# Reordering the products of a fast-matrix-multiply expert loop: y4 placed behind the next pair's two opening products

## The chip, the cores and the metric

The kernel runs on one core of one Trainium2 chip. The time is the device time of one execution in microseconds; shown is the median of several runs. The profile is one further execution, taken by the hardware profiler. TensorE is called PE, VectorE DVE, ScalarE ACT, GpSimd POOL and SyncE SP.

## The reference

A linear attention makes x, and a mixture of eight experts, all of them applied to every token, makes the output:

```python
def _attn_ref(q, k, v):                     # 8 batches, 8 heads, 576 tokens, 64 wide
    q_p, k_p = phi(q), phi(k)               # phi(x) = elu(x) + 1
    kv = np.einsum('bhsd,bhse->bhde', k_p, v)
    num = np.einsum('bhsd,bhde->bhse', q_p, kv)
    den = np.einsum('bhsd,bhd->bhs', q_p, np.sum(k_p, axis=2))[..., None] + 1e-06
    return num / den

def _moe_ref(x, w_gate, w1, w2):            # x 4608 x 512, w1 8 x 512 x 1024, w2 8 x 1024 x 512
    P = np.exp(x @ w_gate - max)            # then 8 rounds of normalising rows and columns
    out = 0
    for e in range(8):
        h = np.maximum(x @ w1[e], 0.0)
        out += P[:, e:e + 1] * (h @ w2[e])
    return out
```

## The kernel before, in words

**Stages.** The attention part, the routing weights P and expert 0 fill the first 206 us. Expert 0 uses plain products of 512 columns (`layer1`, line 546, and `unit_plain`, line 736). Experts 1 to 7 follow. The 4608 tokens are cut into nine groups of 512; one expert on one group is a **unit**, numbered u = 9 e + g, so units 9 to 71 are those of experts 1 to 7. Both layers of a unit are written as a fast matrix multiply in which seven block products take the place of eight. The last unit (71) has the fast form in its first layer only.

**First layer, `block7` (line 603).** It makes h (128 x 8 x 512, f16) in two halves, `pair(0)` and `pair(1)`, called a and b here. Each half has seven products a1 to a7 (b1 to b7). A product is four matmuls of 256 columns, all issued on line 640. Three PSUM banks take the sums:

- X (shown as `hq`, two buffers): product 1, then 6, 7 and 4 on top of it
- R (shown as `att`, two buffers): product 5, then 3
- Z (shown as `Zye`, one bank): product 2 on top of a copy of product 1

Between them ACT copies X after product 1 into Z (the seed, line 652), R after 5 into s5 (line 660) and X after 6 into s2 (line 656), and it makes h11 from Z after 2 (line 663) and h21 from X after 4 (line 666). DVE makes h12 from R and s2 after 3, and h22 from X and s5 after 7 (line 669, issued from lines 672 and 675; the task of h22 is `d22`). Product 4 overwrites what h22 reads, so it waits for h22. DVE also makes the sums W and T of the next expert's weights (lines 783 and 795), one in most units, directly behind h22 of pair b.

**Second layer, `unit` (line 800).** DVE forms four sums S0 to S3 of h (line 816), S0 once all of h is there. Then come seven products y1 to y7 of eight matmuls of 256 columns each (line 843). The bank X of this layer (`ye0`) takes y1, y6, y7 and y4 in that order, R (`ye1`) takes y5 and y3, and Z takes y2 on a copy of y1 (line 878). After y5, y6, y3, y7 and y4 the sum is read out by two DVE instructions each, which add P times it to the output accumulator `acc` (line 857); y2 is read out by ACT into `st` (line 864) and added by POOL (line 867). The next product into the same bank waits for these. y5 needs S0, y6 S1, y7 S2 and y3 S3.

**What sets the order.** Every piece of work is a task of the planner `_Plan` with an estimated time, dependencies, buffers to take and a rank (`prio`, the lowest first). `run()` is a greedy simulation: the engine that can start earliest takes, among the tasks that can start then, the one with the lowest rank, and emits it. So the queue of each engine is fixed when the program is built. On the chip each engine works through its queue and waits on semaphores. Rank for a unit ui: evictions and h11, h12, h21 ui - 400, h22 ui - 402, S ui - 399. On PE the planner has no choice from unit 9 on: `order` (line 919) is a list by hand, and each product is made dependent on the one before it in the list (line 927). A name with y in it means unit u - 1, a and b mean unit u, and a capital A means pair a of unit u + 1. So three units are woven into each other. `final` is the list of the last unit.

**Buffers.** There are two buffers of h. A planner task `tha` (line 612) takes one for a unit. It can be taken when the unit two before has been used for the last time, that is after its last y product. In the kernel before, the first product (`m1`, line 676) waits for `tha` in the plan, although it doesn't touch h. x comes from DRAM in blocks of 896 KB, two buffers, loaded by SP (line 598). The weights are loaded by POOL.

Of the kernel before, what the change touches and what calls it, by code (L numbers as in the profile page):

```python
# [17 lines left out]
class _Plan:  # L18
# [14 lines left out]
    def add(self, eng, fn, deps=(), prio=0.0, acq=(), use=(), lat=0.0, after=0.0):  # L33

        if isinstance(eng, tuple):
            eng = {eng[0]: eng[1]}
        k = len(self.t)
        t = {"eng": eng, "fn": fn, "prio": prio, "acq": tuple(acq), "lat": lat, "kids": [], "nd": 0,
             "ready": after, "done": None, "id": k}
        self.t.append(t)  # L40
        for d in set(x for x in deps if x is not None):
            self.t[d]["kids"].append(k)
            t["nd"] += 1
        for g in list(acq) + list(use):
            g["users"].append(k)
        return k
# [76 lines left out]
def kernel(  # L123
# [28 lines left out]
    add = S_.add  # L152
# [367 lines left out]
    prev_hq = [None]  # L520
# [72 lines left out]
    def x_load(e, g):  # L593
        gr = S_.grp(p_xs)

        def fn(_):
            gr["tile"] = accp[1].tile([P, NXB], FP16, tag="xs", name="xs")
            nc.sync.dma_start(out=gr["tile"], in_=xd[g])
        ti = add(("sp", 0.1), fn, acq=[gr], deps=xd_done[g] + [t_close, xs_prev[0]], prio=e * NG + g)
        xs_prev[0] = ti  # L600
        return gr, add(("dma", 3.0), lambda _: None, deps=[ti], use=[gr], prio=e * NG + g, lat=2.6)

    def block7(e, g, gW, tW):
        gw1, tw1, gw2, tw2 = w_t[e]
        ui = e * NG + g
        gxs, txs = x_load(e, g)
        gh = S_.grp(p_h)
        th = [[], []]

        def f_ha(_):  # L610
            gh["tile"] = hpool.tile([P, NFT, 512], FP16, tag="h", name="h")
        tha = add(("none", 0.0), f_ha, deps=[prev_hq[0]], acq=[gh], prio=ui - 400.0)

        def A(i, j, gi):
            return lambda p, c: gw1["tile"][:, 2 * (j - 1) + c, ts(4 * (i - 1) + 2 * gi + p, P)]

        def W(i, gi):
            return lambda p, c: gW["tile"][:, i - 1, c, ts(2 * gi + p, P)]

        def Bx(o, w):  # L620
            return lambda c: gxs["tile"][:, o + w * c:o + w * c + 256]

        def T(i):
            return Bx(1536 + 512 * (i - 1), 256)
        B11, B21, B22 = Bx(0, 256), Bx(512, 512), Bx(768, 512)

        def pair(gi):
            gX, gR, gZ, gs2, gs5 = (S_.grp(p) for p in (p_hq, p_att, p_ye[3], p_s2, p_s5))
            kx = {id(gX): (hqp, "hq"), id(gR): (aps, "att")}
            f0 = 2 * gi  # L630

            def pm(lhs, rhs, g_, first, deps, pr):
                def f_m(_):
                    if first:
                        pl, tag = kx[id(g_)]
                        g_["tile"] = pl.tile([P, 2, 256], FP32, tag=tag, name=tag)
                    dst = Zt[1] if g_ is gZ else g_["tile"]
                    for p in range(2):
                        for c in range(2):
                            nc.tensor.matmul(dst[:, p, :], lhsT=lhs(p, c), rhs=rhs(c),  # L640
                                             start=(first and p == 0 and c == 0), stop=(c == 1), skip_group_check=True)
                return add(("pe", 0.436), f_m, deps=deps, acq=[g_] if first else [], use=[g_, gw1, gW, gxs],
                           prio=ui + (0.35 if ui > NG else -2.0) + 0.35 * gi + pr)

            def hd(fh, t):
                return gh["tile"][:, 4 * fh + f0:4 * fh + f0 + 2, 256 * t:256 * t + 256]

            def acts(fn, deps, use, acq=()):
                return add(("act", 0.6), fn, deps=deps, use=use, acq=acq, prio=ui - 400.0 + 0.1 * gi)

            def f_seed(_):
                nc.scalar.copy(out=Zt[1], in_=gX["tile"])  # L652

            def f_s2(_):
                gs2["tile"] = accp[2].tile([P, 2, 256], FP32, tag="s2", name="s2")
                nc.scalar.copy(out=gs2["tile"], in_=gX["tile"])  # L656

            def f_s5(_):
                gs5["tile"] = accp[2].tile([P, 2, 256], FP32, tag="s5", name="s5")
                nc.scalar.copy(out=gs5["tile"], in_=gR["tile"])  # L660

            def f_h11(_):
                nc.scalar.activation(out=hd(0, 0), in_=Zt[1], func=AF.Relu)  # L663

            def f_h21(_):
                nc.scalar.activation(out=hd(1, 0), in_=gX["tile"], func=AF.Relu)  # L666

            def addrelu(dst, ps, sb):
                nc.vector._custom_dve(TENSOR_ADD_SAT, out=dst, in0=ps, in1=sb, s0=3.0e38, s1=0.0)  # L669

            def f_h12(_):
                addrelu(hd(0, 1), gR["tile"], gs2["tile"])

            def f_h22(_):
                addrelu(hd(1, 1), gX["tile"], gs5["tile"])
            m1 = pm(A(1, 1, gi), B11, gX, True, tw1 + [tha, txs, prev_hq[0]], 0.0)
            prev_hq[0] = m1
            a1 = acts(f_seed, [m1], [gX], [gZ])
            m5 = pm(W(1, gi), T(1), gR, True, [m1, tW], 0.05)
            a5 = acts(f_s5, [m5, x_closed[0]], [gR], [gs5])  # L680
            m2 = pm(A(1, 2, gi), B21, gZ, False, [a1], 0.15)
            th[0].append(acts(f_h11, [m2], [gZ, gh]))
            m6 = pm(W(2, gi), T(2), gX, False, [a1, tW], 0.08)
            a2 = acts(f_s2, [m6, x_closed[0]], [gX], [gs2])
            m3 = pm(W(4, gi), B22, gR, False, [a5], 0.12)
            th[1].append(add(("dve", 0.69), f_h12, deps=[m3, a2], use=[gR, gs2, gh], prio=ui - 400.0))
            m7 = pm(W(3, gi), T(3), gX, False, [a2], 0.14)
            d22 = add(("dve", 0.69), f_h22, deps=[m7, a5], use=[gX, gs5, gh], prio=ui - 402)
            th[1].append(d22)
            m4 = pm(A(2, 2, gi), T(4), gX, False, [d22], 0.16)  # L690
            for n, t in zip("1234567", (m1, m2, m3, m4, m5, m6, m7)):
                pe_id[(ui, f"{'ab'[gi]}{n}")] = t
            pe_id[(ui, f"{'ab'[gi]}22")] = d22
            th[0].append(acts(f_h21, [m4], [gX, gh]))
        pair(0)
        pair(1)
        return gh, th

# [211 lines left out]
    for e in range(1, E):  # L910
# [3 lines left out]
        for g in range(NG):  # L914
            if e == E - 1 and g == NG - 1:
                unit_plain(e, g, *co[0:2])
            else:
                unit(e, g, *co)
    order = "y1 y5 y2 y6 a7 y3 y7 a4 b1 b5 y4 b6 b3 b2 b7 A1 A5 b4 A6 A3 A2".split()
    final = "y1 y5 y2 y6 a7 y3 a4 b1 b5 y7 b6 b3 b2 b7 y4 b4".split()  # L920
    chain = []
    for u in range(NG - 1, E * NG):
# [83 lines left out]
```

## Time and profile before

| | us |
|---|---|
| median of 11 runs | 977.93 |
| lowest and highest | 976.04, 980.7 |
| profiled execution, its own time | 979.73 |
| profiled execution, span from first to last instruction | 977.9 |
| matmuls of the expert loop (line 843) from, to | 205.9, 966.2 |
| mean granted TensorE clock | 0.998 |

| engine | busy us | share |
|---|---|---|
| PE | 965.2 | 99% |
| PE's weight loads (PEld) | 794.5 | 81% |
| DVE | 768.2 | 79% |
| ACT | 569.3 | 58% |
| POOL | 111.7 | 11% |

The profile gives each instruction a start, a length, the line that issued it and the tiles that it writes and reads (`out<-in`). A matmul's record of 256 columns is 272 ns long, and the next one starts before it ends. Idle time of an engine is listed with what ended it. The chain of waits follows the program back from its last instruction, at each step to what released it.

### The profile page before, as it was taken

What the parts mean: (1) busy time and instruction counts of PE and PEld (TensorE: products, weight loads), DVE (VectorE), ACT (ScalarE), POOL (GpSimd) and SP (SyncE); (2) the same over time, 40 slices, a digit from 0 to 9 for tenths busy, and PEclk for the clock granted to TensorE, in tenths of its full rate; (3) what the DMA queues carried; (4) which work ended last, traced back from release to release, by engine and by line L of the source; (5) the groups of instructions that cost most, each with busy time, mean ns of one, the idle gap of its engine ahead of it and who ended that gap; (6) DMA issues with size and microseconds to landing.
All of it is one profiled execution on the core that took longest, in us unless ns stands there. A gap on an engine that the chain in (4) does not pass through costs nothing.

```text
span 977.9 us, 21442 instructions
## 1 busy us (share of the span) xinstructions
PE 965.2 (99%) x8737; PEld 794.5 (81%) x8737; DVE 768.2 (79%) x1563; ACT 569.3 (58%) x1049; POOL 111.7 (11%) x158
## 2 busy tenths in 40 slices
PE   8899999999999999999999999999999999999998
PEld 4556564588888888888888888888888888888886
DVE  6699868987777777777777777777777777777775
ACT  6699945565555555555555555555555555555553
POOL 3000000101111111111111111111111111111110
PEclk9999999999999999999999999999999999999999
DMA  9886926472226222272226322272225322236664
GB/s 316 231 291 220 252 58 229 157 149 73 73 78 139 93 74 76 73 160 77 76 76 141 95 76 76 77 162 76 77 76 132 107 77 76 76 97 165 161 162 109
DMA packets 47188, 121.99 MB, mean 125 GB/s; under 512 B 4208, under 2 KB 18288, under 8 KB 47088
## 3 DMA queue, kind: packets, MB, share of 16 engines
q1 hardware_dynamic: 32208, 99.76, 30.8%
q0 software_dynamic: 14480, 20.33, 11.7%
q8 instruction: 68, 1.11, 0.5%
q10 hardware_dynamic: 400, 0.52, 0.2%
q14 instruction: 32, 0.26, 0.1%
HBM read 119.69 MB, written 17.69 MB: 140 GB/s over the span
## 4 chain that ended last, share of the span: by engine, by line
PE 91%; DMA 4%; ACT 3%; DVE 1%; issue 1%; POOL 0%; SPq 0%; ACTq 0%; DVEq 0%; POOLq 0%
PE ye L843 33%; PE hq L640 23%; PE att L640 11%; PE ye L736 6%; PE Zye L640 6%; PE Zye L843 6%; PE hq L546 4%; DMA w<-in_moe_w_dram 2%; DMA kin<-in_k_dram 1%; ACT eq L266 1%; PE xt_ps L390 1%; DMA qin<-in_q_dram 1%; PE num_ps L374 1%; ACT h L550 1%; ACT ek L266 0%
## 5 line engine op out<-in xcount | busy, mean ns | idle before, releaser
L857 DVE SCALAR_TENSOR_TENSOR acc<-ye,P_sb,acc 128x256 f32<-128x256 f32 x620 | 264.9, 477 | 95.4 <-PE ye L843 78.7
L640 PEld LDWEIGHTS <-W 128*128 128x128 f16 x2016 | 197.0, 98 | 24.1 <-issue 0.2
L843 PEld LDWEIGHTS <-S 128*128 128x128 f16 x1984 | 194.1, 98 | 22.5
L843 PE MATMUL ye<-T,S 128*128 128x256 f16 x1488 | 192.8, 273 | 0.0
L666 ACT ACTIVATE h<-hq 128x512 f16<-128x512 f32 x126 | 76.4, 606 | 160.1 <-PE hq L640 160.1
L640 PEld LDWEIGHTS <-w 128*128 128x128 f16 x1512 | 147.6, 98 | 23.1 <-issue 0.8
L843 PEld LDWEIGHTS <-h 128*128 128x128 f16 x1488 | 145.6, 98 | 16.9
L867 POOL TENSOR_TENSOR acc<-acc,st 128x256 f32<-128x256 f32 x124 | 87.5, 725 | 625.6 <-ACT st L864 620.7
L640 PE MATMUL hq<-xs,W 128*128 128x256 f16 x1008 | 151.2, 273 | 0.1
L640 PE MATMUL att<-xs,W 128*128 128x256 f16 x1008 | 151.1, 272 | 0.0
L640 PE MATMUL hq<-xs,w 128*128 128x256 f16 x1008 | 140.7, 272 | 0.4 <-DVE h L669 0.3
L816 DVE TENSOR_TENSOR S<-h 128x1024 f16<-128x1024 f16 x124 | 85.3, 688 | 58.2 <-ACT h L666 58.2
L864 ACT ACTIVATE st<-Zye,P_sb 128x256 f32<-128x256 f32 x124 | 52.1, 471 | 78.3 <-PE Zye L843 78.3
L656 ACT COPY s<-hq 128x512 f32<-128x512 f32 x126 | 75.0, 595 | 36.7 <-PE hq L640 36.7
L669 DVE CUSTOM_DVE_ANT_0 h<-att,s 128x512 f16<-128x512 f32 x126 | 86.6, 687 | 11.5 <-ACT s L656 11.0
L663 ACT ACTIVATE h<-Zye 128x512 f16<-128x512 f32 x126 | 75.2, 597 | 34.8 <-PE Zye L640 34.8
L669 DVE CUSTOM_DVE_ANT_0 h<-hq,s 128x512 f16<-128x512 f32 x126 | 86.4, 686 | 0.1
L652 ACT COPY Zye<-hq 128x512 f32<-128x512 f32 x126 | 73.2, 581 | 17.5 <-PE hq L640 17.5
L736 PE MATMUL ye<-w,h 128*128 128x512 f16 x312 | 76.9, 383 | 3.4 <-DMA w<-in_moe_w_dram 2.8
L640 PE MATMUL Zye<-xs,w 128*128 128x256 f16 x504 | 75.6, 273 | 0.0
L660 ACT COPY s<-att 128x512 f32<-128x512 f32 x126 | 74.5, 591 | 0.0
L546 PE MATMUL hq<-xT,w 128*128 128x512 f16 x288 | 70.3, 379 | 1.0 <-ACT h L550 0.8
(95 smaller groups left out, 961.4 us busy)
## 6 DMA issues: line engine op xcount, KB each, us to landing
xs<-xd SPq DMA_DIRECT2D x63, 896.0 KB, 4.6
w<-in_moe_w_dram POOLq DMA_DIRECT2D x14, 1024.0 KB, 11.5
out_dram<-acc SPq DMA_DIRECT2D x67, 128.0 KB, 2.4
kin<-in_k_dram SPq DMA_DIRECT2D x14, 576.0 KB, 5.5
qin<-in_q_dram SPq DMA_DIRECT2D x14, 576.0 KB, 5.5
vin<-in_v_dram SPq DMA_DIRECT2D x14, 576.0 KB, 6.1
xd<-xst SPq DMA_DIRECT2D x9, 512.0 KB, 2.8
xd<-xT SPq DMA_DIRECT2D x9, 256.0 KB, 3.2
```

What stands on the lines that cost most here:

```text
L546: nc.tensor.matmul(ghq["tile"], lhsT=gw1["tile"][:, c, ts(f, P)], rhs=xT[:, c, ds(512 * g, 512)], start=(c == 0), stop=(c == NDT - 1))
L640: nc.tensor.matmul(dst[:, p, :], lhsT=lhs(p, c), rhs=rhs(c), start=(first and p == 0 and c == 0), stop=(c == 1), skip_group_check=True)
L656: nc.scalar.copy(out=gs2["tile"], in_=gX["tile"])
L660: nc.scalar.copy(out=gs5["tile"], in_=gR["tile"])
L663: nc.scalar.activation(out=hd(0, 0), in_=Zt[1], func=AF.Relu)
L666: nc.scalar.activation(out=hd(1, 0), in_=gX["tile"], func=AF.Relu)
L669: nc.vector._custom_dve(TENSOR_ADD_SAT, out=dst, in0=ps, in1=sb, s0=3.0e38, s1=0.0)
L736: nc.tensor.matmul(gy[tt]["tile"], lhsT=gh["tile"][:, f, ds(P * tt, P)], rhs=gw2["tile"][:, f, :], start=(f == 0), stop=(f == NFT - 1))
L816: nc.vector.tensor_tensor(out=Sx[:, i], in0=a0, in1=a1, op=op)
L843: nc.tensor.matmul(bank(g_)[:, s, :], lhsT=lhs(s, kk), rhs=rhs(kk), start=(new and s == 0 and kk == 0), stop=(kk == 3), skip_group_check=True)
L857: nc.vector.scalar_tensor_tensor(out=dst(), in0=bank(g_)[:, s, :], scalar=P_sb[:, gg, e:e + 1], in1=dst(), op0=ALU.mult, op1=ALU.add)
L867: nc.gpsimd.tensor_tensor(out=dst(), in0=dst(), in1=gst["tile"], op=ALU.add)
```

## The change

The list `order` is made anew. Three things move in it: y4 of the unit before goes from behind b5 to behind A5 (of the next unit); y7 goes from behind y3 to behind b5; a7 goes in front of y6. a4 follows y3 directly then. `final` stays as it is. With this list A1 of unit u + 1 comes ahead of y4 of unit u - 1, whose h buffer it would have to wait for in the plan. So `m1` no longer depends on `tha`; the four tasks that write h (`f_h11`, `f_h12`, `f_h22`, `f_h21`) do in its place.

```diff
-            m1 = pm(A(1, 1, gi), B11, gX, True, tw1 + [tha, txs, prev_hq[0]], 0.0)
+            m1 = pm(A(1, 1, gi), B11, gX, True, tw1 + [txs, prev_hq[0]], 0.0)
...
-            th[0].append(acts(f_h11, [m2], [gZ, gh]))
+            th[0].append(acts(f_h11, [m2, tha], [gZ, gh]))
...
-            th[1].append(add(("dve", 0.69), f_h12, deps=[m3, a2], use=[gR, gs2, gh], prio=ui - 400.0))
+            th[1].append(add(("dve", 0.69), f_h12, deps=[m3, a2, tha], use=[gR, gs2, gh], prio=ui - 400.0))
...
-            d22 = add(("dve", 0.69), f_h22, deps=[m7, a5], use=[gX, gs5, gh], prio=ui - 402)
+            d22 = add(("dve", 0.69), f_h22, deps=[m7, a5, tha], use=[gX, gs5, gh], prio=ui - 402)
...
-            th[0].append(acts(f_h21, [m4], [gX, gh]))
+            th[0].append(acts(f_h21, [m4, tha], [gX, gh]))
...
-    order = "y1 y5 y2 y6 a7 y3 y7 a4 b1 b5 y4 b6 b3 b2 b7 A1 A5 b4 A6 A3 A2".split()
+    order = "y1 y5 y2 a7 y6 y3 a4 b1 b5 y7 b6 b3 b2 b7 A1 A5 y4 b4 A6 A3 A2".split()
     final = "y1 y5 y2 y6 a7 y3 a4 b1 b5 y7 b6 b3 b2 b7 y4 b4".split()
```

## The prediction

> **What bounds the kernel now.** I read the page first (engine shares, then the chain that ended last), then the waits of PE, then the chain in a steady stretch, then the timeline of one unit.
>
> ```profile
> PE 965.2 (99%) x8737; PEld 794.5 (81%) x8737; DVE 768.2 (79%) x1563; ACT 569.3 (58%) x1049; POOL 111.7 (11%) x158
> ...
> PE 91%; DMA 4%; ACT 3%; DVE 1%; issue 1%; POOL 0%; SPq 0%; ACTq 0%; DVEq 0%; POOLq 0%
> ```
>
> PE sets the end: 91% of the chain. But 99% busy does not say that it runs at its rate, since one matmul's record (272 ns) is longer than the distance to the next. For the same reason the waits of PE name almost nothing of the expert loop; a hold shorter than that overlap is no gap there:
>
> ```profile
> PE ye L736 <- DMA w<-in_moe_w_dram: 2.8, 2, 2.7
> ...
> PE hq L640 <- DVE h L669: 0.3, 1, 0.3
> ```
>
> So I looked at distances between starts. In the chain from 410 to 452 us each piece is listed with its length; eight matmuls of 256 columns take 0.87 us, but one piece in each unit takes 0.94:
>
> ```profile
> 411.94 0.87 PE hq L640 x8
> ...
> 413.25 0.94 PE hq L640 x8
> ...
> 425.55 0.94 PE hq L640 x8
> ...
> 437.84 0.94 PE hq L640 x8
> ...
> 450.14 0.94 PE hq L640 x8
> ```
>
> The distance is 12.30 us, one unit. The timeline of the last one (start, length, engine) says which product is late and on what:
>
> ```profile
> 448.67 0.60 PE L640 MATMUL hq<-xs,W 128*128 128x256 f16 x4
> ...
> 449.10 0.60 PE L640 MATMUL hq<-xs,w 128*128 128x256 f16 x4
> 449.30 0.69 DVE L669 CUSTOM_DVE_ANT_0 h<-hq,s 128x512 f16<-128x512 f32 x1
> ...
> 449.54 0.60 PE L640 MATMUL att<-xs,W 128*128 128x256 f16 x4
> ...
> 449.87 0.50 PEld L640 LDWEIGHTS <-w 128*128 128x128 f16 x4
> ...
> 450.05 0.60 PE L640 MATMUL hq<-xs,w 128*128 128x256 f16 x4
> ```
>
> These are b7, A1, A5 and b4. Products of four matmuls lie 0.44 us apart, A5 to b4 is 0.51. b7 starts at 448.67, DVE's h22 of pair b (line 675) can start at 449.30, ends at 449.99, and b4, which overwrites the bank that h22 reads, starts 0.06 us later. A1 and A5 cover 0.87 us of that chain, which needs 0.94. From the individual matmul starts in the trace the hold is 0.071 to 0.075 us in each of the 61 units after the first: 61 x 0.072 = 4.4 us. Everything else in the loop (206 to 966 us) that exceeds the 0.109 us pace sums to 0.8 us: 0.21 and 0.07 once at 549 us, 0.49 in the last unit at 961 us.
>
> The first unit of expert 1 is a control inside this trace: there a plain second-layer product (line 736) stands between b7 (201.86) and A1.
>
> ```profile
> 201.86 0.60 PE L640 MATMUL hq<-xs,W 128*128 128x256 f16 x4
> ...
> 202.30 1.03 PE L736 MATMUL ye<-w,h 128*128 128x512 f16 x4
> ...
> 203.60 0.60 PE L640 MATMUL att<-xs,W 128*128 128x256 f16 x4
> ...
> 204.03 0.60 PE L640 MATMUL hq<-xs,w 128*128 128x256 f16 x4
> ```
>
> A5 to b4 is 0.43 there: no hold.
>
> [...] b4's first weight load (449.87) is on time, 0.11 us ahead of the slot 449.98; only the matmul is held; and DVE shows the same order in every unit, apart from the extra W and T sums. [...]
>
> **The change part by part.** I count slots from y1 = 0, with 0.873 for a y product and 0.437 for an a, b or A product. New: y5 0.87, y2 1.75, a7 2.62, y6 3.06, y3 3.93, a4 4.80, b1 5.24, b5 5.68, y7 6.11, b6 6.98, b3 7.42, b2 7.86, b7 8.29, A1 8.73, A5 9.17, y4 9.60, b4 10.48, A6 10.91, A3 11.35, A2 11.79, next y1 12.22. No instruction is added or removed; at the pace a unit is 12.22 us against 12.30.
>
> 1. *y4 from behind b5 to behind A5.* The cover of h22 becomes 1.75 us: b4 could start at 8.29 + (450.05 − 448.67 = 1.38) = 9.67, its slot is 10.48; margin 0.81. Gain 61 x 0.072 = **4.4 us**.
> What is late next? In the old order two holds stand just behind: A6 (450.48) waits for ACT's seed copy from A1 (ends 450.36), A3 (450.92) for the s5 copy from A5 (ends 450.87). At 205.00 A3 is indeed 0.07 late. Both sit behind y4 now and gain 0.87 us less the 0.07; nothing is late there.
> y4's own followers: its two evictions on DVE begin 1.08 us after its first matmul (446.48 to 447.56) and take 0.88 for both. Now 10.68 to 11.56; y1 needs the bank at 12.22: margin 0.6 where it was 3.3. On DVE they are queued in front of the first S sum, which waits for ACT's h21 of pair b (old: start at 451.40, 0.39 before y1, after 0.81 idle). The new evictions end at 11.56, S starts at about 11.83, so they fill that idle time and delay nothing. A W or T sum (0.68), in 48 of 54 units of experts 1 to 6, goes directly behind h22, at about 9.5 to 10.2, still before them. If this cover is gone, each 0.1 us beyond the margin costs 6 us.
> 2. *y7 into y4's old place.* y7's two evictions take exactly the place of y4's in front of h12 and h22 of pair b (a gap of 0.18 us on DVE stays), so b6 to b7 run as before. y7 needs y6's evictions (4.14 to 5.02), due 6.11: margin 1.1, before 0.2. y4 needs y7's (7.19 to 8.07), due 9.60. No cost.
> 3. *a7 in front of y6, a4 in front of y7.* y6 comes 0.44 later: its inputs are easier. a7 comes 0.87 earlier: it needs A6's s2 copy, issued a product group before y1; no cost. h22 of pair a becomes ready at 2.62 + 0.65 = 3.27. S3, the last S sum, which y3 (3.93) waits for, runs 2.81 to 3.49 in the old trace. h22 follows it 0.60 later, 3.41 to 4.10; a4 is due 4.80: margin 0.65. That rests on S3 staying ahead in DVE's queue (rival 2).
> 4. *h taken by the first write.* Only the planner sees it: A1 no longer has to be placed behind y4 of the unit before, without which the order could not be made. The writers of h follow A2, A3, a7 and a4, and PE has passed y4 by then; no new wait. At the start of expert 1 the planner may place A1 one y half (0.87) earlier among products that keep PE full either way; I bound that by the holds seen there (0.02 and 0.07) and the same again as a loss: ±0.1, taken as 0.
> 5. *Queues passed.* SP: the load of x for unit u+2 goes out when b4 of unit u ends (450.68) and must land by A1 at 461.4; it takes 4.6 us. A1 comes 0.9 earlier: margin 5. POOL: its adds follow y2, which does not move; the weight loads for w2 wait for y4, 2.6 us later once per expert, with an expert's time (110 us) to land. Expert 7's output transfers come 2.6 us later except those of the last unit, whose order is unchanged. Nothing on the path.
>
> Sum: 4.4, and 0.2 for the hold at 549 us (A6, a rare late ACT start of 0.28, which the wider cover would absorb): 4.5 us to one figure after the point, bounds 4.2 to 5.0. Profiled execution: span 977.9 becomes 973.4, and with the 1.8 us outside the span 979.7 becomes 975.2. The median of the runs, 977.93, lies 1.8 below the profiled execution; I take the difference over: **973.4**.
>
> **Rivals.**
> 1. *The wait moves on.* A hold of about 0.07 per unit appears at another product (A3 at 205.00 shows how near it lies): 61 x 0.07 back, 977.7. Against it: y4 stands in front of A6 and A3 too. 8%.
> 2. *h22 of pair a gets ahead of S3 on DVE.* It has the higher rank (ui − 402 against ui − 399), so the planner takes it first if both are ready. DVE would then run it at 3.27 and S3 at 3.88 to 4.56; y3 would start at 4.61, not 3.93: 61 x 0.68 = 41 us, 1015. It decides where the planner has S3 later than h22's readiness. By the plan's own constants h21 ends 11.71, so S0 starts at 11.77, then h12 12.37, S1 12.98, S2 13.67, two evictions to 15.07, S3 at 15.07; h22 is ready at 12.22 + 3.06 + 0.2 = 15.47: 0.4 us to spare, and the order before it is that of the old trace. 5%.
> 3. *y4's evictions reach y1.* A further 0.7 to 0.8 us in front of them, as a W or T sum queued there, would eat the margin and hold y1 by some 0.1 to 0.2 us in 48 units: 5 to 10 us, 978 to 983. Against it: that sum is ready a whole us earlier. 4%.
>
> **How the numbers follow.** Forecast 83%, rivals 8, 5 and 4%. About 0.2% (2 us, below 975.97) is what can be told from no change. Runs of before spread over 976.0 to 980.7, so I give a median about 1 us either way. Range: 4.4 plus all 0.8 of the other holds, and 0.5 of spread, gives 972.2 below; above, I go to 976.2, where 60% of the gain is lost, toward rival 1. Same is rival 1 and half of rival 3, slower rival 2 and the other half: faster 0.83, same 0.10, slower 0.07.
>
> **What would show it.** Right: A5, y4, b4 at the pace, and no piece of 0.94 in the chain; y1 to y1 at 12.22; DVE's idle time before the first S sum (58.2 us in all) shrunk. Step 1 wrong: y1 more than 0.44 behind A2's start. Step 3 wrong: y3 more than 0.88 behind y6, with h22 in front of S3. Step 4 wrong: A1's first matmul held. The prediction is wrong if unit distances stay at 12.30.

## The result, and the profile after

The changed kernel takes 972.59 us (median of 13 runs), the kernel before 978.51 us in the same comparison (50 runs). The ratio is 0.9944 with a 95% interval of 0.993 to 0.9958; of 978.5 us that is 5.5 us less (4.1 to 6.9); the two medians themselves lie 5.9 us apart. A second comparison with new runs gave 0.9952 (0.9933 to 0.9971), 4.7 us. The forecast was 4.5 us less, and 973.4 us in a range of 972.2 to 976.2.

The page after, shares and chain:

```profile
PE 959.6 (99%) x8737; PEld 794.5 (82%) x8737; DVE 776.6 (80%) x1563; ACT 574.9 (59%) x1049; POOL 111.7 (12%) x158
...
PE 93%; ACT 3%; DVE 2%; DMA 1%; issue 0%; ACTq 0%; DVEq 0%
```

The work is the same (the counts of instructions are), and PE still sets the end. As before, the shares don't tell what changed. The chain in a steady stretch does (start, length, piece):

```profile
421.67 1.75 PE ye L843 x16
...
429.96 0.87 PE hq L640 x8
430.83 0.44 PE att L640 x4
431.27 0.87 PE ye L843 x8
432.14 0.87 PE hq L640 x8
...
433.89 1.75 PE ye L843 x16
```

A piece is counted from the end of the one before it, so b4, whose first matmul starts at 431.98, is in the piece listed at 432.14, where y4's last record ends. That piece is 0.87 us long where it was 0.94, and from one y1 to the next it is 12.22 us where it was 12.30. The timeline of that unit shows why (start, length, engine):

```profile
429.80 0.60 PE L640 MATMUL hq<-xs,W 128*128 128x256 f16 x4
...
430.44 0.69 DVE L669 CUSTOM_DVE_ANT_0 h<-hq,s 128x512 f16<-128x512 f32 x1
...
430.67 0.60 PE L640 MATMUL att<-xs,W 128*128 128x256 f16 x4
...
431.11 1.04 PE L843 MATMUL ye<-T,h 128*128 128x256 f16 x8
...
431.98 0.60 PE L640 MATMUL hq<-xs,w 128*128 128x256 f16 x4
432.18 0.88 DVE L857 SCALAR_TENSOR_TENSOR acc<-ye,P_sb,acc 128x256 f32<-128x256 f32 x2 [0.46 <-PE ye L843]
...
433.25 0.69 DVE L816 TENSOR_TENSOR S<-h 128x1024 f16<-128x1024 f16 x1 [0.19 <-ACT h L666]
...
433.73 1.04 PE L843 MATMUL ye<-w,h 128*128 128x256 f16 x8
```

b7 starts at 429.80 and h22 of pair b still ends 1.33 us later, at 431.13; but b4 is now due at 431.98, because y4 stands in between. y4's evictions (432.18 to 433.06) lie in the time in which DVE waited for h21 before; that wait ahead of S0 is 0.19 us in this unit, where it was 0.81. Over the whole program the page lists 12.3 us of it, before 58.2.

Cut into three by the starts of the first and the last matmul of line 843, the profiled executions stand so:

| | front | loop | tail | span |
|---|---|---|---|---|
| before | 205.87 | 760.31 | 11.73 | 977.9 |
| after | 201.42 | 755.81 | 11.74 | 969.0 |

The loop is 4.50 us shorter. The front is 4.45 us shorter too, so that these two executions differ by 8.9 us; the experiments show that this second part doesn't belong to the change.

### The profile page after: what moved, and what is told of

It is laid out like the page before. It is cut to its first block, busy times and chain, and to the rows that moved or that the text cites. A ratio compares the mean times of both kernels' runs of the same rounds, so it can differ in the third digit from the quotient of the medians.

```text
span 969.0 us, 21442 instructions
## 1 busy us (share of the span) xinstructions
PE 959.6 (99%) x8737; PEld 794.5 (82%) x8737; DVE 776.6 (80%) x1563; ACT 574.9 (59%) x1049; POOL 111.7 (12%) x158
## 4 chain that ended last, share of the span: by engine, by line
PE 93%; ACT 3%; DVE 2%; DMA 1%; issue 0%; ACTq 0%; DVEq 0%
PE ye L843 33%; PE hq L640 23%; PE att L640 11%; PE ye L736 6%; PE Zye L640 6%; PE Zye L843 6%; PE hq L546 4%; PE yw L481 1%; DMA kin<-in_k_dram 1%; PE xt_ps L390 1%; ACT eq L266 1%; PE kv_ps L309 1%; ACT h L550 1%; PE num_ps L374 1%; PE qt_ps L335 0%
## 5 line engine op out<-in xcount | busy, mean ns | idle before, releaser
L816 DVE TENSOR_TENSOR S<-h 128x1024 f16<-128x1024 f16 x124 | 85.4, 688 | 12.3 <-ACT h L666 12.3
```

The lines of the kernel that those rows point to most:

```text
L816: nc.vector.tensor_tensor(out=Sx[:, i], in0=a0, in1=a1, op=op)
```

## The experiments

The loop is a good measure, since it repeats to 0.01 us, and the holds in it can be read from the distances of matmul starts: everything above 0.109 us. The holds in the last unit and the two at 549 us are not in the table. Each experiment had one profiled execution; the last two kernels were also timed in five rounds. All changes are to the changed kernel. Where a new `order` is shown with a plus, it stands in place of the changed kernel's.

| run | front | loop | holds per unit (61 units) |
|---|---|---|---|
| before, again | 202.23 | 760.30 | b4 0.072 |
| h part alone | 206.51 | 760.31 | b4 0.072 |
| y4 alone | 202.18 | 788.54 | b6 0.465, b3 0.078 |
| no swap of y6 and a7 | 201.83 | 785.20 | a4 0.485 |
| y4 in front of A1 | 201.98 | 760.22 | A3 0.069 |
| S3 behind h22 | 202.07 | 808.99 | y3 0.856 |
| S3 behind h22, POOL held | 203.28 | 797.56 | y3 0.675 |
| y4 behind A6 | 201.96 | 776.52 | y1 0.269, b4 0.071 |
| after, again | 204.60 | 755.81 | none |
| swap in the last list too | 202.47 | 755.32 | none |

**The kernel before, again.** No edit.

> The kernel before, unchanged, profiled once more. Measured in each run: the loop (first to last matmul of the second layer, 760.3 us before, 755.8 after) and the front (what lies ahead of it, 205.9 before, 201.4 after). My theory: the loop is fixed by the queues, so 760.3 again with 61 holds of 0.07 at b4; the front is the same program in both kernels and varies from run to run, so anything from 201 to 206. Rival (the change shortened the front): front near 205.9 again, and near 201.4 only with the change.

Loop 760.30, the same 61 holds, the same single ones. The front came out at 202.23 where it had been 205.87 with the very same program; the changed kernel gave 201.42 and 204.60. So the front varies by several microseconds on its own. All engines go through the same instructions in the same order (by line and tiles) in both kernels until 208.4 us, where the new list first differs. What varies is, first, how long PE waits. In the first profile of before PE waited 2.8 us for expert 0's weights; in this one (what waited, for what: total, times, longest):

```profile
PE ye L736 <- DMA w<-in_moe_w_dram: 1.4, 1, 1.4
```

In the first profile of after there is no such wait, in the second it is 2.2 us. The arrival of that transfer is not all of it. The longest front, 206.51 us in the run of the next paragraph, has 2.8 us of waiting for an ACT instruction at 108 us. And the longest waits came with a second loss. Of the stretch from 15 to 45 us, the first profile of before and this one show (length, then busy time of PE, PEld, DVE, ACT and POOL, then the granted clock, DMA share and GB/s):

```profile
15.00:45.00 30.00, 25.42 (x241) 14.44 (x236) 20.91 (x48) 18.17 (x30) 3.65 (x5) 0.94 1.00 304
...
15.00:45.00 30.00, 26.67 (x289) 15.78 (x284) 24.09 (x54) 21.10 (x34) 3.67 (x5) 1.00 1.01 305
```

The 0.94 is a stretch of 3.41 us at clock 0.5, begun 0.6 us after PE's longest wait (2.68 us) ended. The same 3.41 us at 0.5 follow the wait of 2.24 us in the second profile of after and that of 2.78 us in the run of the h part. In the other nine profiles, where no wait of PE in the front is longer than 2.07 us, the clock does not drop there. The three with the drop have the three longest fronts, 204.6 to 206.5 us; the other nine lie between 201.4 and 203.3. By an estimate from the trace, half speed for 3.41 us costs 1.7 us.

**The h part alone.**

```diff
-    order = "y1 y5 y2 a7 y6 y3 a4 b1 b5 y7 b6 b3 b2 b7 A1 A5 y4 b4 A6 A3 A2".split()
+    order = "y1 y5 y2 y6 a7 y3 y7 a4 b1 b5 y4 b6 b3 b2 b7 A1 A5 b4 A6 A3 A2".split()
```

> Old order of products, h taken by its first write. My theory: this part only makes the new order possible; loop 760.3, b4 held 0.07 in 61 units. Rival (the looser taking of h is where the gain comes from): loop near 755.8.

Loop 760.31, b4 held as before. The looser taking of h gives nothing by itself; the rival falls. The trace shows why: every engine has the same instructions in the same order as in the kernel before. The part only makes the new order possible.

**y4 alone.**

```diff
+    order = "y1 y5 y2 y6 a7 y3 y7 a4 b1 b5 b6 b3 b2 b7 A1 A5 y4 b4 A6 A3 A2".split()
```

> y4 behind A5 as in the new order, but y7, y6 and a7 stay in their old places, so that b6 follows b5 directly. My theory: b4 is unheld, but b1 to b3 now has no y product in it, and that chain (b1, seed copy, s5 copy, b3) needs 1.84 us by the old trace's A1 to A3 at 203.16 to 205.00, against a slot of 1.31: b6 held 0.45 and b3 some 0.08, 0.53 in each of 61 units, loop 788. Rival (only y4's move counts): loop 755.8.

Loop 788.54: b4 is free, but the gap that y4 leaves behind b5 is worth seven times what it fills. The chain shows both holds (start, length, piece): a4, then h21 and b1's seed copy on ACT, then b6 and b3:

```profile
437.76 0.45 PE hq L640 x4
...
438.23 0.60 ACT h L666
438.83 0.50 ACT Zye L652
...
439.37 0.60 PE hq L640 x4
439.97 0.51 PE att L640 x4
```

The seed copy of b1 (line 652) comes directly behind h21 on ACT, and b6 waits for it; b3 (0.51, not 0.44) then waits for the s5 copy. From b1's start (438.03) to b3's (439.88) it is 1.85 us, as the 1.84 of the expectation. So y7's move into that place is no decoration: it pays for y4's.

**No swap of y6 and a7.**

```diff
+    order = "y1 y5 y2 y6 a7 y3 a4 b1 b5 y7 b6 b3 b2 b7 A1 A5 y4 b4 A6 A3 A2".split()
```

> y4 and y7 moved, but y6 stays in front of a7. My theory: between a7 and a4 stands y3 alone (0.87 us), and h22 of pair a waits on DVE behind the two evictions of y6, as in the last unit of the old trace, where a4 is held 0.49: 0.49 in each of some 61 units, loop 785.5. Rival (the swap is of no account): loop 755.8.

Loop 785.20, a4 held 0.485. DVE's timeline shows h22 of pair a (447.85) behind the two evictions of y6 (447.05), and a4 behind it (the last line holds a4 and b1):

```profile
447.05 0.88 DVE L857 SCALAR_TENSOR_TENSOR acc<-ye,P_sb,acc 128x256 f32<-128x256 f32 x2 [0.34 <-ACT st L864]
...
447.85 0.68 DVE L669 CUSTOM_DVE_ANT_0 h<-hq,s 128x512 f16<-128x512 f32 x1
...
448.58 1.03 PE L640 MATMUL hq<-xs,w 128*128 128x256 f16 x8 [0.32 <-DVE h L669]
```

So y4's move pays only together with the two others.

**y4 in front of A1.** The cover between b7 and b4 is the same, the place is not.

```diff
+    order = "y1 y5 y2 a7 y6 y3 a4 b1 b5 y7 b6 b3 b2 b7 y4 A1 A5 b4 A6 A3 A2".split()
```

> The new order with y4 in front of A1 and not behind A5. h22 of pair b has the same cover of 1.75 us, but A1, A5, b4, A6, A3 follow one another as in the old order. My theory: b4 unheld, and the wait moves to A6 and A3: A1 to A3 needs 1.84 us against a slot of 1.75, 0.09 in each unit, loop 761.3, no better than before. Rival (any place between b7 and b4 serves): loop 755.8. Second rival (b4 pays a fixed price for following A5): b4 still 0.07 late, loop 760.3.

Loop 760.22. b4 is free, so it pays no fixed price for its place, and the wait has moved to A3, as this run's theory and the prediction's first rival had it. A1, A5, s5, A3 in its timeline:

```profile
445.19 0.60 PE L640 MATMUL hq<-xs,w 128*128 128x256 f16 x4
445.62 0.60 PE L640 MATMUL att<-xs,W 128*128 128x256 f16 x4
...
446.36 0.59 ACT L660 COPY s<-att 128x512 f32<-128x512 f32 x1
...
447.00 0.60 PE L640 MATMUL att<-xs,W 128*128 128x256 f16 x4
```

A1 to A3 is 1.81 us against a slot of 1.75. I had expected 0.09 per unit; it is 0.069, all at A3 (nothing is held at A6, where I had put 0.02). This is the run that says why y4 has to stand behind A5: there one product covers two chains, b7 to b4 and A1 to A3.

**y4 behind A6.**

```diff
+    order = "y1 y5 y2 a7 y6 y3 a4 b1 b5 y7 b6 b3 b2 b7 A1 A5 b4 A6 y4 A3 A2".split()
```

> y4 two products later, behind b4 and A6. My theory: b4 is held 0.07 and A6 0.02 again, and y1 waits for y4's evictions: 1.08 + 0.88 + 0.05 = 2.01 us from y4's start, against 0.87 + 0.87 of slots, 0.27 more: 0.35 in each unit, loop 777. Rival (the evictions at the unit's end are hidden): only 0.07 to 0.09, loop 760 to 761.

Loop 776.52. From y4's start (451.17) to y1's (453.19) it takes 2.02 us; y1 is held 0.269. So y4's evictions are not hidden for free: the margin in the changed kernel, 0.6 us, is used up two products later. b4 is held by 0.071 again, since A1 and A5 alone cover its chain.

**S3 behind h22 of pair a.** The slower rival of the prediction, made real by one dependency in the plan:

```diff
+        pe_id[(ui, "s3")] = tS[3]
...
+    for u in range(NG + 1, E * NG - 1):
+        S_.dep(pe_id[(u - 1, "s3")], pe_id[(u, "a22")])
```

> The new order, with S3 queued on DVE behind h22 of pair a (the slower rival of the prediction made real by one dependency in the plan). My theory: y3 is held 0.68 in each of 61 units, loop 755.8 + 41 = 797. If the price was mis-sized (the hold passed on and partly absorbed): less, down to 0.4 per unit, 780.

Loop 808.99, 53.2 us more; y3 is held 0.856, not 0.68. The timeline shows what I had left out: S3 takes 0.87 us, and of POOL's two adds the first takes 0.72 and the second 1.16.

```profile
441.03 0.69 DVE L669 CUSTOM_DVE_ANT_0 h<-hq,s 128x512 f16<-128x512 f32 x1 [0.43 <-PE hq L640]
...
441.24 0.72 POOL L867 TENSOR_TENSOR acc<-acc,st 128x256 f32<-128x256 f32 x1 [9.50 <-ACT st L864]
...
441.64 0.87 DVE L816 TENSOR_TENSOR S<-h,S 128x1024 f16<-128x1024 f16 x1
...
441.93 1.16 POOL L867 TENSOR_TENSOR acc<-acc,st 128x256 f32<-128x256 f32 x1
...
442.56 1.05 PE L843 MATMUL ye<-w,S 128*128 128x256 f16 x8 [0.70 <-DVE S L816]
```

Alone, S3 takes 0.68 and each add 0.73, the pair 1.41. In these lines S3 and the adds run at the same time, so I tried the overlap by itself.

**S3 behind h22, POOL held.** A small copy on POOL that reads S3 keeps the adds back (62 copies of four columns are added work). Its edit is that of the run before, and:

```diff
+        def f_hold(_):
+            nc.gpsimd.tensor_copy(out=gate, in_=gS["tile"][:, 3, 0, 0, 0:4])
+        hold = add(("pool", 0.15), f_hold, deps=[tS[3]], use=[gS], prio=ui - 400.5)
+        for s in range(2):
+            S_.dep(fin_prev[(4 * g + 2 * s, 0)], hold)
```

> As e5_s3_behind, but a small copy on POOL that reads S3 (added work, four columns) holds POOL's two adds of y2 back until S3 is done. In e5_s3_behind S3 took 0.86 us, not 0.68, while those adds ran beside it (1.86 us for both, not 1.41). My theory: the overlap with POOL is the 0.18 that the price lacked: S3 is back at 0.68, the hold of y3 at 0.68, loop 755.8 + 41 = 797. Rival (S3 is long because it follows h22 directly on DVE): S3 stays 0.86, loop 809.

Loop 797.56, y3 held 0.675. S3 starts 0.61 us behind h22, as in the run before, and is back at 0.68:

```profile
438.94 0.69 DVE L669 CUSTOM_DVE_ANT_0 h<-hq,s 128x512 f16<-128x512 f32 x1 [0.39 <-PE hq L640]
...
439.55 0.68 DVE L816 TENSOR_TENSOR S<-h,S 128x1024 f16<-128x1024 f16 x1
...
440.37 0.18 POOL L887 CAST gate<-S 128x4 f32<-128x4 f16 x1 [10.48 <-DVE S L816]
440.53 1.41 POOL L867 TENSOR_TENSOR acc<-acc,st 128x256 f32<-128x256 f32 x2
```

So the missing 0.18 was the overlap with POOL. The three lines of the run before show which instruction got longer. The first add, which started before S3, kept its length (0.72); S3, which started during it, got 0.18 longer (medians of the loop, 0.86 for 0.68); and the second add, which started during S3, took 1.16, and the pair of adds 0.45 longer (1.86 for 1.41). Why it is the later one each time, the traces don't show.

**The changed kernel, again, and the swap in the last list.** The second one's edit:

```diff
-    final = "y1 y5 y2 y6 a7 y3 a4 b1 b5 y7 b6 b3 b2 b7 y4 b4".split()
+    final = "y1 y5 y2 a7 y6 y3 a4 b1 b5 y7 b6 b3 b2 b7 y4 b4".split()
```

> The changed kernel unchanged, timed in five rounds beside the kernel before on this chip, and profiled once more. My theory: loop 755.8, front anywhere from 201 to 206, ratio to before 0.995 (4.7 us of loop over 978). Rival (the change also shortens the front by 4.5): ratio 0.9906, front near 201.4.

> The changed kernel with the last unit's list given the same swap (a7 in front of y6). My theory: the one hold that is left in the loop (0.49 at a4 of the last unit) goes, loop 755.3, nothing else; in the time that can't be told from the changed kernel. Rival: another wait takes its place in the last unit, loop 755.8.

Changed kernel: loop 755.81 again, ratio to before 0.9952 (0.9933 to 0.9971), with a front of 204.60. The interval leaves out the rival's 0.9906. With the last list swapped: loop 755.32 and no distance between matmul starts above 0.110 us left in it, ratio 0.9953 (0.9939 to 0.9966). The two can't be told apart in the time, as expected for 0.5 us.

## Why the prediction was right, step by step

**The bound and the hold.** Right. The loss was in matmul starts and not in the waits; 61 holds of 0.072 are gone and nothing took their place. Loop 760.31 to 755.81, 4.50 us, forecast 4.5. The traces show that the stream keeps to 109 ns, and that no distance in it is under 108 ns; whether it could be shorter was not shown.

**Step 1, y4.** Right in sign, size and margins. h22's end to b4's slot is 0.85 us in the unit shown, 0.8 after the handover of 0.05 (the median from h22's end to a held b4 in before is 0.054; forecast 0.81). y4's evictions end 0.67 before y1, 0.6 with the handover (forecast 0.6), and moving y4 on made them late by the 0.27 that their sum of 2.01 gave. S0 was forecast at 11.83 after y1 and came at 11.75. A2 to y1 is 0.44 in every unit. That A3 is next in line and gains from the same y4 is shown by the run with y4 in front of A1; A6, named with it, was not held there. The late ACT start, 0.21 of hold at 549 us before, is there again at 541 us after and holds nothing; with it went the 0.07 at A3 behind it, which the sum had left out.

**Step 2, y7.** No cost, as forecast. What the prediction said too little of is that the step is needed: without it b6 and b3 lose 0.54 per unit.

**Step 3, a7 and a4.** No cost; S3 stayed ahead of h22 in the queue (436.47 and 437.07 in the timeline after). The swap is worth 0.485 per unit.

**Step 4, h.** The part alone gives 0.00, and leaves every queue as it was. The possible move of A1 at the start of expert 1 didn't take place: PE's queue is the same in both kernels up to y2 of unit 9.

**Sum and median.** The loop gave 4.50, but that this is the forecast's 4.5 to the last figure is luck. The sum's own terms, 4.4 and 0.2, make 4.6. By the traces 4.41 us of holds went at b4 and 0.28 at 549 us, 4.69 in all; against it, the three distances inside a held b4 are 108 ns and not 109, which gives back 3 ns in each of 61 units, 0.18 us. The first comparison shows 5.5 (interval 4.1 to 6.9), the second 4.7 (2.8 to 6.6); both hold 4.5, and neither holds 8.9. The rest of the 8.9 us between the two profiled executions lies in the front, which varies from 201.4 to 206.5 us over twelve profiles: with the old order it is 202.2 to 206.5, with the changed kernel 201.4 and 204.6.

**Rivals.** The first is real in another place (y4 in front of A1). The second was a price only, and the price was mis-sized: 0.68 per unit left out the overlap with POOL, 0.18; 41 us should have been 53. The third did not occur.

## What to carry to other kernels

Where an engine is listed as 99% busy, measure the distance between starts of like instructions: a hold shorter than the overlap of two records (0.16 us here) appears in no list of waits, and repeated 61 times it is nearly the whole gain. Cost a reordering as chains (producer's start to the follower's earliest start, 1.38, 1.81 and 2.02 us here) against the slots between them, for the step that moves, for the place that it leaves and for its own followers. One piece of independent work placed behind the starts of two chains covers both; here, two products earlier, it covered only one. Before two profiles are compared by their whole spans, cut them where the change begins: 4.45 of the 8.9 us between these two lay ahead of it.

## What the runs showed of the hardware that was not expected

The hold of a queue-bound loop repeats to a few nanoseconds: 0.070 to 0.075 in each of 61 units, and the loop of 760 us to 0.01 us between executions. Two ACT instructions start 0.28 us late, near 549 and 713 us in before and at the same two places of the program in after and in each repeat of both; the place is fixed, the cause isn't shown. An f16 subtraction of two SBUF operands on DVE went from 0.68 to 0.86 us (medians) when it started during an f32 add on POOL, and an add that started during the subtraction took 1.16 in the unit shown, and 1.18 at most, where adds take 0.73 by themselves; the add that came first took 0.72. The granted clock fell to 0.5 for 3.41 us after waits of PE of 2.24, 2.68 and 2.78 us, and not after one of 2.07; whether the length of the wait decides it isn't shown.
